# Longer runs in the loads of v and q, the weights' loads on SyncE's queue, and a reciprocal root in eight instructions, in an attention and channel-mixing kernel on one core

## The chip, the cores and the metric

The kernel runs on one core of one Trainium2 chip. The metric is the device time of one execution in microseconds, as the median of several runs. One core has TensorE (PE, with weight loads shown as PEld), VectorE (DVE), ScalarE (ACT), GpSimd (POOL), and SyncE (SP), which here only issues DMAs. SP's and ACT's queues both feed the core's 16 DMA engines.

## What is computed

Normalized attention over 8 batches, 12 heads, 448 positions and 64 columns per head, and then a channel-mixing block on the attention's output x of width 768, with inner width 1024:

```python
q_n, k_n = rmsnorm(q, g_q), rmsnorm(k, g_k)        # x / sqrt(mean(x*x) + 1e-6) * g
scores = (q_n @ k_n.T) / 8
attn = exp(scores - max) / (sum + 1e-9)
x = (attn @ v), heads side by side                 # (8, 448, 768)
x_prev = x shifted by one position
xk, xr = mu_k * x + (1 - mu_k) * x_prev, mu_r * x + (1 - mu_r) * x_prev
k = relu(xk @ w_k);  out = sigmoid(xr @ w_r) * ((k * k) @ w_v)
```

q, k, v and the g factors arrive as float32, the weights and mu as float64. The result is float32.

## The kernel before, in words

**Units.** The heads of a batch are worked in pairs (48 in all, `pairs`) and quads of four heads (24, `quads`, u in the code). Position p of a head is split as p = 7 r + t: r (0 to 63) lies on a partition, and t (0 to 6) in the free dimension. Two heads share the 128 partitions.

**Precision.** Numbers that go through PE are split into a high and a low float16 part, and three products are added up (high by high, high by low, low by high). The first batch's attention (quads 0 to 2, `U32 = 3`) is done in float32 in place of that, with one product. The weights are turned from float64 to float32 by bit operations, scaled per column block by a power of two, and split.

**Steps of a quad.** `load` fetches k and q into tiles `qk` (in part lent room named `xk`). `stats` squares them on ScalarE into a `nat` tile, GpSimd adds the halves, VectorE reduces to 28 sums per partition (`sst`), scales them, and `rsqrt` computes the reciprocal root (`ss`, with `stm` as room) by a bit trick and three Newton steps. `preps` multiplies by it. For quads 0 to 5 (`PE_T = 6`), PE transposes the result (`turn`), and the copy out of PSUM multiplies k by the factor g, held as a column `gc`; from quad 6 on GpSimd multiplies by g (`G`), ScalarE and GpSimd write the high and low part, and a DMA transpose brings them into `stk`. g_q, g_k and the 1/8 are folded into one factor, which is scaled by a number `gm` so that its largest element is balanced; the same number goes into q's root.

**Attention.** `scores` makes groups of 128 query rows by 448 keys in PSUM (`sc`), `expo` takes the maximum on VectorE and the exponential on ScalarE, `split` writes high and low part into `nat`, and a DMA transpose (or PE, in every other of the first groups, `probs_pe`) brings them into `pT`. `vload` fetches v of one pair (`vf`, two buffers) by four loads, `vprep` finds its scale (square, maximum over partitions by one small matmul, exponent bits) and writes high and low part (`vh`, `vl`). `attends` multiplies `pT` by v and copies the result out of PSUM into `x`.

**Channel mixing.** `wload` fetches forty half column blocks of the weights into `raw` (or lent room named `kk`), `weights` and `wsplit` convert them. `mix` forms xk and xr, `moe` multiplies, `square`, `gate` and `store` finish and write out. The first batch's `moe` cannot begin before the first weights are ready, and not end before all are.

**Order.** All of this is written as generators. A planner (`Plan`) holds a model of each engine's clock, of the DMAs and of each tile's last use; at each step it picks the generator whose next instruction could start first, less a priority (`PRIO_...`, `BOOST_...`, `MARGIN...`), and fixes that order on every engine. So the program is one static list for each engine. A waiting instruction holds all behind it on its engine, and a DMA that waits holds all behind it on its queue. Since all operations are issued by one helper, the profile gives nearly all of them the line L272.

In the kernel before, SP issues the loads of k, q and v, the transposes and the stores; ACT issues three of the first quad's loads, the forty weights' loads and the two of mu.

Of the kernel before, what the change touches and what calls it, by code (L numbers as in the profile page):

```python
# [16 lines left out]
P = 128  # L17
# [7 lines left out]
NH = D_MODEL // 2  # L25
TINY = 2.0 ** -60
RELU_SCALE = 2.0 ** -23.5
NEWTON = 3
# [12 lines left out]
VF_BUFS = 2  # L41
# [4 lines left out]
PRIO_P = 200  # L46
PRIO_S = 150
PRIO_A = 50
PRIO_Q = 50
PRIO_V = 310  # L50
MARGIN = 600
MARGIN_A = 400
MARGIN_V = 1200
# [5 lines left out]
PRIO_O = 300  # L59
# [3 lines left out]
BOOST_R = 500  # L63
BOOST_A = 0
BOOST_W = 300
BOOST_Q = 600
SLACK_S = 3
SLACK_Q = 2
# [6 lines left out]
PRIO_L = 0  # L75
# [3 lines left out]
V_SIDE = 2  # L79
SWITCH = 600  # L80
# [5 lines left out]
BOOST_F = 4000  # L86
# [8 lines left out]
W_GAP = 10e3  # L95
W_PUSH = 0.03
NEWTON_ON = "DVE"
# [18 lines left out]
def heads(tile_, off):  # L116
    ap = tile_[:, :, :]
    return bass.AP(tensor=ap.tensor, offset=ap.offset + off, ap=[list(ap.ap[0]), [HD, 2], [2 * HD, NT], [1, HD]])
# [86 lines left out]
class Plan:  # L205
    LAT = 35

    def __init__(self, tc):
        self.tc = tc
        self.clk = dict.fromkeys(("PE", "DVE", "ACT", "POOL", "SP"), 0.0)  # L210
        self.last, self.use, self.threads = {}, {}, []
        self.form, self.dma_free, self.acc, self.n = None, {"SP": 0.0, "ACT": 0.0}, False, 0
        self.held = {"DVE": [], "POOL": []}

# [51 lines left out]
    def emit(self, ops):  # L266
# [18 lines left out]
        elif ops[0].fn.__name__.startswith("dma"):  # L285
            op = ops[0]
            x = op.kw["out"]
            n = width(x) * x.ap[0][1]
            if "transpose" in op.fn.__name__:
                w, iss, tot = n / 128 * 1.21, 1600, 4000  # L290
            else:
                w, iss, tot = n / 55, 640, 3300
            w, tot = w * DMA_SLOW, tot * DMA_SLOW
            other = "ACT" if e == "SP" else "SP"
            if e == "ACT":
                end = s + (375 if n > 60000 else 610)
            else:
                end = max(s + iss, min(self.dma_free[e] - 1200, s + 4000))
# [5 lines left out]
            self.note(op, self.dma_free[e] + 900)  # L304
        else:
# [99 lines left out]
def rsqrt(V, y, a, t, pool=None):  # L405
    ti = t.bitcast(I32)
    yield V.tensor_scalar(out=ti, in0=a.bitcast(I32), scalar1=1, scalar2=None, op0=ALU.logical_shift_right)
    yield V.tensor_scalar(out=y.bitcast(I32), in0=ti, scalar1=-1.0, scalar2=float(0x5F3759DF), op0=ALU.mult, op1=ALU.add)
    for _ in range(NEWTON):
        if pool:  # L410
            yield pool.tensor_tensor(out=t, in0=a, in1=y, op=ALU.mult)
            yield pool.tensor_tensor(out=t, in0=t, in1=y, op=ALU.mult)
            yield pool.tensor_scalar(out=t, in0=t, scalar1=-0.5, scalar2=1.5, op0=ALU.mult, op1=ALU.add)
            yield pool.tensor_tensor(out=y, in0=t, in1=y, op=ALU.mult)
        else:
            yield V.tensor_tensor(out=t, in0=a, in1=y, op=ALU.mult)
            yield V.scalar_tensor_tensor(out=t, in0=t, scalar=-0.5, in1=y, op0=ALU.mult, op1=ALU.mult)
            yield V.scalar_tensor_tensor(out=y, in0=t, scalar=1.5, in1=y, op0=ALU.add, op1=ALU.mult)


def attn_moe_kernel(tc, q, k, v, g_q, g_k, mu_k, mu_r, w_k, w_v, w_r, out):
# [22 lines left out]
    gc = const.tile([P, 1], F32, name="gc")  # L444
# [8 lines left out]
    ones = const.tile([P, 1], F32, name="ones")  # L453
    WS = {}
# [4 lines left out]
    NQ, NPAIR, NSS, NSL = len(quads), len(pairs), 4 * NT, (NT + 1) // 2  # L459
    VFREE = [const.tile([P, 2 * NSL, HD], F32, name="vf%d" % n) for n in range(VF_BUFS)]  # L460

# [17 lines left out]
    def late():  # L479
# [11 lines left out]
        "vh": Ring(ap_, [P, 2 * NSL, HD], F16, "vh", VH_BUFS, plan),  # L491
        "vl": Ring(ap_, [P, 2 * NSL, HD], F16, "vl", VH_BUFS, plan),
# [39 lines left out]
    def setup():  # L532
        yield SP.dma_start(out=gq, in_=g_q.partition_broadcast(P))
        yield SP.dma_start(out=gk, in_=g_k.partition_broadcast(P))
        yield A.copy(out=ident16, in_=ident)
        yield V.memset(out=ones, value=1.0)
        for vf in VFREE:
            yield G_.memset(out=vf[HD:P, NSL - 1, :], value=0.0)
            yield G_.memset(out=vf[0:HD, NSL, :], value=0.0)
        st["vf"] = True  # L540
        yield V.scalar_tensor_tensor(out=G, in0=gq, scalar=1.0 / float(HD) ** 0.5, in1=gk, op0=ALU.mult, op1=ALU.mult)
        yield V.tensor_reduce(out=gm[:, 0:1], in_=G, axis=AX.X, op=ALU.max, apply_absolute_value=True)
# [3 lines left out]
        for h in range(2):  # L546
            hs = slice(h * HD, (h + 1) * HD)
            yield V.tensor_tensor(out=gd[hs, :], in0=G[hs, :], in1=ident[hs, hs], op=ALU.mult)
        yield V.tensor_reduce(out=gc, in_=gd, axis=AX.X, op=ALU.add)
        yield V.tensor_tensor(out=gm[:, 2:3], in0=gm[:, 1:2], in1=gm[:, 1:2], op=ALU.mult)  # L550
        yield V.tensor_scalar(out=gm[:, 3:4], in0=gm[:, 2:3], scalar1=1.0 / HD, scalar2=None, op0=ALU.mult)
        yield V.tensor_scalar(out=gm[:, 4:5], in0=gm[:, 2:3], scalar1=1e-6, scalar2=None, op0=ALU.mult)
        st["gm"] = True

    def mu_stats():
        yield from until(lambda: st["lu"] >= 1 and len(WFT))
        yield A.dma_start(out=mu[:, 0, 0, :], in_=mu_k.rearrange("(t p) -> p t", p=P))
        yield A.dma_start(out=mu[:, 1, 0, :], in_=mu_r.rearrange("(t p) -> p t", p=P))
        yield V.tensor_scalar(out=mu[:, :, 1, :], in0=mu[:, :, 0, :], scalar1=-1.0, scalar2=1.0, op0=ALU.mult, op1=ALU.add)
        u = small.tile([P, 2, ND], F32, name="muu")  # L560
        u2 = small.tile([P, 2, ND], F32, name="muu2")
        col = small.tile([P, 2], F32, name="mucol")
# [6 lines left out]
        m = small.tile([P, 1], F32, name="allmax")  # L569
# [7 lines left out]
    def load():  # L577
        for u in range(NQ):
# [3 lines left out]
            for n, src in enumerate((k, q)):  # L582
                t = yield from R["qk"].get(u < 3)
                for x in range(2):
                    D = (A if u == 0 and (x or n == 0) else SP).dma_start
# [3 lines left out]
                    else:  # L589
                        tf = t.rearrange("p h c -> p (h c)")  # L590
                        for t0 in range(x, NT - 1, 2):
                            o = t0 // 2 * 4 * HD
                            yield D(out=tf[x * HD:(x + 1) * HD, o:o + 4 * HD].rearrange("p (h d) -> p h d", d=HD),
                                    in_=src[b, 4 * j:4 * j + 4].rearrange("h (r t) d -> r h t d", t=NT)[:, :, t0, :])
                        yield D(out=tf[x * HD:(x + 1) * HD, 12 * HD:].rearrange("p (h d) -> p h d", d=HD),
# [7 lines left out]
    def stats():  # L603
        for u in range(NQ):
            st["su"] = u
            yield from until(lambda: u in LD and (st["gm"] or u < PE_T))
            y = small.tile([P, NSS], F32, name="ss", bufs=3)
            ss = small.tile([P, NSS], F32, name="sst", bufs=3)
            tm = small.tile([P, NSS], F32, name="stm", bufs=3)
            for n, t in enumerate(LD[u]):  # L610
# [3 lines left out]
                yield A.activation(out=xs, in_=tv, func=AF.Square)  # L614
# [8 lines left out]
            yield from rsqrt(V, y, ss, tm, NEWTON_ON == "POOL" and G_)  # L623
            SS[u] = y

    def preps():
        for u in range(NQ):
# [4 lines left out]
            for n, t in enumerate(LD.pop(u)):  # L632
# [13 lines left out]
                nat = yield from R["nat"].get(u < 3)  # L646
                if n:
# [6 lines left out]
                R["qk"].put(t)  # L654
                yield SP.dma_start_transpose(out=X[:, n], in_=nat.rearrange("p a c -> p (a c)"))
                R["nat"].put(nat)
            TQ[u] = X
            st["tq"] = u + 1

    def turn(w, X, n, u):  # L660
# [554 lines left out]
```

## Time and profile before

| what | value |
|---|---|
| median of 3 runs | 1036.73 us (1035.93 to 1038.05) |
| the profiled execution, first to last instruction | 1038.0 us |
| PE busy | 935.8 us, 90% of the span |
| VectorE busy | 788.0 us, 76% |
| ScalarE busy | 749.4 us, 72% |
| GpSimd busy | 661.0 us, 64% |
| mean granted TensorE clock | 0.970 |
| DMA packets | 447,043, of them 418,784 under 512 B |

How to read it: the span is that of the one profiled execution, from 0 to 1038.0 with 0.24 us ahead of its first instruction; it stands beside the longest of the three runs (1038.05), 1.3 us above their median. A busy share over the whole span is a mean over stages that have different limits. Idle time in front of an instruction is put down to what released it last. Matmuls overlap each other, so their summed durations are more than PE's busy time.

### The profile page before, as it was taken

The numbers are of one execution on the slowest core, as the hardware profiler recorded it, in microseconds if no ns is written. First come the engines' busy times: TensorE is split into PE (matmuls) and PEld (weight loads), VectorE is DVE, ScalarE is ACT, GpSimd is POOL, SyncE is SP. The second block draws the span as 40 slices with busy tenths as digits, with TensorE's granted clock in tenths as the row PEclk, the third lists the DMA queues.
The fourth block names the chain that finished last, engine by engine and source line by source line (L and its number), as shares of the span: only waits on it lengthen the run. The fifth ranks groups of instructions, "written<-read, shape, count | busy, mean of one in ns | idle before, by whom it ended". The sixth has DMA issues, their size and how long they took to land. (4 is left out here: it accounts for less than half of the span.)

```text
span 1038.0 us, 19082 instructions
## 1 busy us (share of the span) xinstructions
PE 935.8 (90%) x6262; PEld 495.5 (48%) x6262; DVE 788.0 (76%) x1973; ACT 749.4 (72%) x1755; POOL 661.0 (64%) x696
## 2 busy tenths in 40 slices
PE   1778677879999999999999999899989999999997
PEld 1444433435554555454545544455545554555564
DVE  4898879998978897978895988779876879673000
ACT  2787657997968887888887886987887787873311
POOL 2564658936678567877677757855984757646501
PEclk9898887989999999999999999999999999999999
DMA  8543437988897999789798798799869977771011
GB/s 198 143 122 106 115 91 166 202 160 155 156 174 125 176 183 161 139 156 179 157 175 140 152 185 167 129 171 183 173 118 159 170 154 135 139 140 32 1 31 31
DMA packets 447043, 146.63 MB, mean 141 GB/s; under 512 B 418784, under 2 KB 443360, under 8 KB 446944
## 3 DMA queue, kind: packets, MB, share of 16 engines
q1 hardware_dynamic: 427408, 127.42, 65.7%
q10 hardware_dynamic: 19536, 18.00, 6.1%
q8 instruction: 49, 0.80, 0.3%
q14 instruction: 50, 0.41, 0.1%
HBM read 50.40 MB, written 11.01 MB: 59 GB/s over the span
## 5 line engine op out<-in xcount | busy, mean ns | idle before, releaser
L272 PE MATMUL mm<-wvh,kk 128*128 128x384 f16 x896 | 233.8, 326 | 0.6 <-POOL kk L272 0.4
L272 ACT ACTIVATE sc<-sc,sums 128x448 f32<-128x448 f32 x294 | 180.9, 617 | 59.2 <-DVE sums L272 54.8
L272 DVE TENSOR_REDUCE sums<-sc 128x1 f32<-128x448 f32 x336 | 194.8, 614 | 28.7 <-PE sc L272 27.9
L272 PE MATMUL mm<-xk,wkh 128*128 128x448 f16 x768 | 209.0, 354 | 3.8 <-ACT kf L272 2.6
L272 DVE SCALAR_TENSOR_TENSOR nat<-sc,sums,nat 128x448 f16<-128x448 f32 x246 | 161.2, 675 | 29.1 <-ACT nat L272 28.6
L272 ACT ACTIVATE nat<-sc,sums 128x448 f16<-128x448 f32 (+1 forms) x278 | 168.7, 648 | 14.2 <-DVE sums L272 4.9
L272 PE MATMUL mm<-wrh,xr 128*128 128x384 f16 x672 | 177.6, 329 | 0.0
L272 PEld LDWEIGHTS <-kk 128*128 128x128 f16 (+1 forms) x1362 | 129.5, 98 | 96.3 <-issue 14.4
L272 PE MATMUL sc<-stk 64*128 64x448 f16 (+3 forms) x1104 | 131.7, 385 | 22.1 <-DVE nat L272 12.7
L272 PE MATMUL mm<-wvl,kk 128*128 128x384 f16 x448 | 146.0, 326 | 0.0
L272 PE MATMUL mm<-xk,wkl 128*128 128x448 f16 x384 | 135.8, 354 | 0.0
L272 PEld LDWEIGHTS <-xr 128*128 128x128 f16 x1008 | 96.1, 98 | 73.9 <-issue 14.4
L272 PE MATMUL ot<-pT,vh 128*64 128x448 f16 x672 | 103.3, 364 | 11.1 <-DMA pT<-nat 7.4
L272 PE MATMUL mm<-wrl,xr 128*128 128x384 f16 x336 | 110.3, 328 | 0.0
L272 PEld LDWEIGHTS <-wkh 128*128 128x128 f16 x768 | 72.1, 98 | 79.1 <-issue 18.4
L272 DVE SCALAR_TENSOR_TENSOR o<-o,mm 128x384 f32<-128x384 f32 x56 | 30.7, 548 | 88.5 <-PE mm L272 58.5
L272 POOL TENSOR_TENSOR o<-o,bsc 128x384 f32<-128x384 f32 x48 | 42.9, 894 | 82.0 <-DVE o L272 49.3
L272 POOL TENSOR_TENSOR qk<-qk,ss 128x896 f32<-128x896 f32 x36 | 63.3, 1757 | 44.4 <-DVE ss L272 36.7
L272 ACT ACTIVATE o<-mm,bsc 128x128 f32<-128x128 f32 x144 | 44.6, 382 | 50.8 <-PE mm L272 38.6
L272 PEld LDWEIGHTS <-stk 64*128 64x128 f16 x1008 | 36.1, 98 | 80.2 <-issue 50.7
L272 DVE SCALAR_TENSOR_TENSOR df<-x,bsc,df 128x448 f32<-128x448 f32 x68 | 63.2, 941 | 5.4 <-POOL df L272 5.3
L272 POOL TENSOR_TENSOR nat<-nat 128x448 f32<-128x448 f32 x38 | 44.5, 1170 | 35.1 <-ACT nat L272 35.0
(169 smaller groups left out, 1784.5 us busy)
## 6 DMA issues: line engine op xcount, KB each, us to landing
out_dram<-o SPq DMA_DIRECT2D x56, 192.0 KB, 3.3
qk<-in_k_dram SPq DMA_DIRECT2D x46, 224.0 KB, 3.8
qk<-in_q_dram SPq DMA_DIRECT2D x108, 64.0 KB, 2.5
vf<-in_v_dram SPq DMA_DIRECT2D x96, 64.0 KB, 2.7
raw<-in_moe_w_v_dram ACTq DMA_DIRECT2D x12, 512.0 KB, 4.9
vf<-in_v_dram SPq DMA_DIRECT2D x96, 48.0 KB, 2.4
raw<-in_moe_w_r_dram ACTq DMA_DIRECT2D x12, 384.0 KB, 3.4
kk<-in_moe_w_k_dram ACTq DMA_DIRECT2D x8, 384.0 KB, 4.4
```

The costliest lines, as they stand in the source:

```text
L272: r = op.fn(op.kw["out"], op.kw["value"]) if op.fn.__name__ == "memset" else op.fn(**op.kw)
```

## The change

- **v**: loaded, squared and scaled by quads and not by pairs, from quad 3 on with one scale for the quad. One buffer `vf` of double size takes the place of two. Each load takes four or three neighbouring t of a row of the split (1024 or 768 B in one run) where it took single ones (256 B). High and low part of a pair lie in one tile, `vhl`.
- **q from quad 6 on**: three neighbouring t of a head in one run (768 B), and the seventh by itself; four loads a quad, not eight.
- To keep the columns in step, `turn`, the high and low parts in `preps`, and the copy in `attends` use another order of t; the latter two need two instructions where there was one.
- **Queues**: the weights' and mu's loads, and q's second half of quad 0, are issued by SP. The loads of g_q and g_k come after those of the first quad.
- **g**: in batch 0 (quads 0 to 2) the factor is used without the balancing number, so `stats` of these quads does not wait for it.
- **Root**: `rsqrt` in eight instructions, not eleven; the scaling of the sums is done in the Square, and one addition of `eps` is left.
- The small tiles `ss`, `sst`, `stm` and `dg` come from rings that the planner knows; the planner gets a limit of eight DMAs in flight, other DMA costs, and other priorities.

```diff
-VF_BUFS = 2
+VF_BUFS = 1
...
-W_GAP = 10e3
+W_GAP = 6679.939
 class Plan: def emit
+            if len(self.flying) == DMA_LANES:
+                s = max(s, self.flying.pop(0))
...
-def rsqrt(V, y, a, t, pool=None):
...
+def rsqrt(V, y, a, t):
+    yield V.tensor_scalar(out=y.bitcast(I32), in0=a.bitcast(I32), scalar1=-0.5, scalar2=float(0x5F3759DF), op0=ALU.mult, op1=ALU.add)
+    yield V.tensor_tensor(out=t, in0=a, in1=y, op=ALU.mult)
+    yield V.tensor_tensor(out=t, in0=t, in1=y, op=ALU.mult)
+    yield V.scalar_tensor_tensor(out=t, in0=t, scalar=-10.0 / 3, in1=t, op0=ALU.add, op1=ALU.mult)
+    yield V.scalar_tensor_tensor(out=y, in0=t, scalar=5.0, in1=y, op0=ALU.add, op1=ALU.mult)
+    yield V.tensor_tensor(out=t, in0=a, in1=y, op=ALU.mult)
+    yield V.scalar_tensor_tensor(out=t, in0=t, scalar=-27.0 / 1024, in1=y, op0=ALU.mult, op1=ALU.mult)
+    yield V.scalar_tensor_tensor(out=y, in0=t, scalar=9.0 / 16, in1=y, op0=ALU.add, op1=ALU.mult)
 def setup
+        yield from until(lambda: 0 in LD)
         yield SP.dma_start(out=gq, in_=g_q.partition_broadcast(P))
         yield SP.dma_start(out=gk, in_=g_k.partition_broadcast(P))
...
+        yield V.tensor_reduce(out=gc[:, 0:1], in_=gd, axis=AX.X, op=ALU.add)
+        st["gc"] = True
...
+        yield V.tensor_tensor(out=gc[:, 1:2], in0=gc[:, 0:1], in1=gm[:, 1:2], op=ALU.mult)
 def mu_stats
-        yield A.dma_start(out=mu[:, 0, 0, :], ...
+        yield SP.dma_start(out=mu[:, 0, 0, :], ...
 def load
-                    D = (A if u == 0 and (x or n == 0) else SP).dma_start
+                    D = (A if u == 0 and n == 0 else SP).dma_start
...
-                        for t0 in range(x, NT - 1, 2):
-                            o = t0 // 2 * 4 * HD
-                            yield D(out=tf[x * HD:(x + 1) * HD, o:o + 4 * HD].rearrange("p (h d) -> p h d", d=HD),
-                                    in_=src[b, 4 * j:4 * j + 4].rearrange("h (r t) d -> r h t d", t=NT)[:, :, t0, :])
+                        w = NLO * HD
+                        yield D(out=tf[xs, 0:4 * w].rearrange("p (h c) -> p h c", h=4),
+                                in_=src[b, 4 * j:4 * j + 4].rearrange("h (r t) d -> r h (t d)", t=NT)[:, :, x * w:(x + 1) * w])
 def stats
-                yield A.activation(out=xs, in_=tv, func=AF.Square)
+                yield A.activation(out=xs, in_=tv, func=AF.Square, scale=gm[:, 6:7] if n and u >= U32 else HD ** -0.5)
...
-            yield from until(lambda: st["gm"])
-            yield V.tensor_scalar(out=ss[:, 0:2 * NT], in0=ss[:, 0:2 * NT], scalar1=1.0 / HD, scalar2=1e-6, op0=ALU.mult, op1=ALU.add)
-            yield V.tensor_scalar(out=ss[:, 2 * NT:NSS], in0=ss[:, 2 * NT:NSS], scalar1=gm[:, 3:4], scalar2=gm[:, 4:5], op0=ALU.mult, op1=ALU.add)
+            if u < U32:
+                yield V.tensor_scalar(out=ss, in0=ss, scalar1=1e-6, scalar2=None, op0=ALU.add)
+            else:
+                yield from until(lambda: st["gm"])
+                yield V.tensor_tensor(out=ss, in0=ss, in1=eps, op=ALU.add)
 def preps
-                yield A.copy(out=hi, in_=t4)
-                yield E_.tensor_tensor(out=lo, in0=t4, in1=hi, op=ALU.subtract)
+                for t4, hi, lo in views:
+                    yield A.copy(out=hi, in_=t4)
+                for t4, hi, lo in views:
+                    yield E_.tensor_tensor(out=lo, in0=t4, in1=hi, op=ALU.subtract)
 def vload
-        for i in range(NPAIR):
+        for u in range(NQ):
...
-                    yield SP.dma_start(out=vf[e * HD:(e + 1) * HD, o:o + n, :], in_=src[h][:, t::2, :])
+                    yield SP.dma_start(out=vf[e * HD:(e + 1) * HD].rearrange("p (x c) d -> p x (c d)", x=2)[:, :, o * HD:(o + n) * HD],
+                                       in_=src[:, :, t * HD:(t + n) * HD])
 def vprep
+        if half:
+            hl = yield from R["vhl"].get()
+            yield A.activation(out=hl.rearrange("p a c d -> p (a c) d").bitcast(BF16), in_=vf, func=AF.Square, accum_out=vs[:, 0:1])
...
+            for e in range(2):
+                if e:
+                    hl = yield from R["vhl"].get()
+                ve = vf[:, 2 * NSL * e:2 * NSL * (e + 1), :]
+                yield A.activation(out=hl[:, 0], in_=ve, func=AF.Copy, scale=sv)
+                yield V.scalar_tensor_tensor(out=hl[:, 1], in0=ve, scalar=sv, in1=hl[:, 0], op0=ALU.mult, op1=ALU.subtract)
 def attends
-            for lo, hi in ((0, NT),) if i % 2 == 0 else ((NT - 1, NT), (0, NT - 1)):
...
+            yield A.activation(out=x[:, 1:NT, :].rearrange("p (a t) c -> p t a c", a=2), in_=av[:, o:o + (NT - 1) * HD].rearrange("p (t a c) -> p t a c", a=2, c=HD), func=AF.Copy, ...
+            yield A.activation(out=x[:, NT, :], in_=av[:, o:o + HD], func=AF.Copy, ...
 def wload
-                yield A.dma_start(out=raw[:, 0:hk, :], in_=w[i * P:(i + hk) * P, ...
+                yield SP.dma_start(out=raw[:, 0:hk, :], in_=w[i * P:(i + hk) * P, ...
```

The rest of the constants, not shown: `PRIO_P` 200 to 429, `PRIO_S` 150 to 159, `PRIO_A` 50 to 37, `PRIO_V` 310 to 295, `MARGIN` 600 to 560, `MARGIN_A` 400 to 305, `MARGIN_V` 1200 to 569, `PRIO_O` 300 to 161, `PRIO_L` 0 to 165, `BOOST_R` 500 to 816, `BOOST_W` 300 to 248, `BOOST_Q` 600 to 898, `SLACK_S` 3 to 4, `SLACK_Q` 2 to 3, `SWITCH` 600 to 404, `BOOST_F` 4000 to 3894. A priority counts a tenth of its value in nanoseconds (`PS = 0.1`); `W_GAP` is the pace, in nanoseconds per column block, at which the weights' priority rises.

More of the change, by code (lines that the diff above doesn't have):

```diff
@@ L25 @@
 NH = D_MODEL // 2
+NSL = (NT + 1) // 2
+NLO = NT // 2
+KORD = [t // 2 + NSL * (t % 2) for t in range(NT)]
+QORD = [t // 2 + NLO * (t % 2) for t in range(NT - 1)] + [NT - 1]
 TINY = 2.0 ** -60
 RELU_SCALE = 2.0 ** -23.5
-NEWTON = 3
+DMA_LANES = 8
 MX = 4 + 2 * ND
@@ L606, in stats @@
             yield from until(lambda: u in LD and (st["gm"] or u < PE_T))
-            y = small.tile([P, NSS], F32, name="ss", bufs=3)
-            ss = small.tile([P, NSS], F32, name="sst", bufs=3)
-            tm = small.tile([P, NSS], F32, name="stm", bufs=3)
+            ss = yield from R["sst"].get()
             for n, t in enumerate(LD[u]):
@@ L711, in vfree @@
+            VF[u] = vf
+    def vfree(u, vf):
+        FR[u] = FR.get(u, 0) + 1
+        if FR[u] == 3:
             VFREE.append(vf)
     def vpreps():
-        i = 0
-        while i < NPAIR:
-            st["vi"] = i
-            n = V_SIDE if i < 2 * U32 else 1
-            yield from vprep([i + e for e in range(n)])
-            i += n
-    def vprep(js):
-        b, hp = pairs[js[0]]
-        n, half = len(js), js[0] >= 2 * U32
-        if hp == 0:
-            BS[b] = small.tile([P, 2 * NP], F32, name="bstat", bufs=3)
+        for u in range(NQ):
+            st["vi"] = u
+            yield from vprep(u)
@@ L726, in vprep @@
+    def vprep(u):
+        b, j = quads[u]
+        half = u >= U32
+        n = 1 if half else 2
+        NS = NP // 2 * n
+        if j == 0:
+            BS[b] = small.tile([P, 2 * NS], F32, name="bstat", bufs=3)
         s_ = BS[b]
         vs = small.tile([P, 4], F32, name="vs", bufs=4)
-        vh = vl = pt = None
-        for e, i in enumerate(js):
-            yield from until(lambda: i in VF and st["tq"] >= GATE_V)
-            vf = VF.pop(i)
-            if half:
-                vh = yield from R["vh"].get()
-                vl = yield from R["vl"].get()
-                sq = vh.bitcast(BF16)
-            else:
-                VV[i] = vf, None, None
-                pt = pt or (yield from banks["ot"].get())
-                sq = pt.rearrange("p (a c) -> p a c", c=HD)
-            yield A.activation(out=sq, in_=vf, func=AF.Square, accum_out=vs[:, e:e + 1])
-            if not half:
-                vfree(i, vf)
-                if e < n - 1:
-                    banks["ot"].put(pt)
-                    pt = None
@@ L746, in vprep @@
-        pt = pt or (yield from banks["ot"].get())
+        yield from until(lambda: u in VF and st["tq"] >= GATE_V)
+        vf = VF.pop(u)
+        hl = pt = None
+        if half:
+            hl = yield from R["vhl"].get()
+            yield A.activation(out=hl.rearrange("p a c d -> p (a c) d").bitcast(BF16), in_=vf, func=AF.Square, accum_out=vs[:, 0:1])
+            pt = yield from banks["ot"].get()
+        else:
+            for e in range(2):
+                VV[2 * u + e] = vf[:, 2 * NSL * e:2 * NSL * (e + 1), :], None, vf
+            pt = yield from banks["ot"].get()
+            for e in range(2):
+                yield A.activation(out=pt.rearrange("p (a c) -> p a c", c=HD), in_=vf[:, 2 * NSL * e:2 * NSL * (e + 1), :], func=AF.Square, accum_out=vs[:, e:e + 1])
+            vfree(u, vf)
@@ L1041, in wsplit @@
         sci = sc.bitcast(I32)
-        dg = small.tile([P, P], F32, name="dg", bufs=1)
+        dg = yield from R["dg"].get()
         yield V.tensor_tensor(out=dg, in0=pg[:, 0:P], in1=ident, op=ALU.mult)
         yield T.matmul(form=("f", 400), out=pg[:, P:2 * P], lhsT=ones.broadcast_to([P, P]), rhs=dg, start=True, stop=True)
+        R["dg"].put(dg)
         yield V.tensor_reduce(out=sc, in_=pg[:, P:2 * P], axis=AX.X, op=ALU.max)
```

190 lines of the change are left out of this document (96 added, 94 removed).

## The prediction

> **What bounds the kernel now.** I read the page first, then the busy time by stages, then PE's waits in the steady stage, then the first 25 us instruction by instruction, and last the groups of VectorE inside the front stage alone. The page gives the span, the packets, and the queue that nearly all of them are on (packets, MB, share of 16 DMA engines over the span):
>
> ```profile
> span 1038.0 us, 19082 instructions
> ...
> DMA packets 447043, 146.63 MB, mean 141 GB/s; under 512 B 418784, under 2 KB 443360, under 8 KB 446944
> ...
> q1 hardware_dynamic: 427408, 127.42, 65.7%
> ```
>
> The stages (length, then busy us of PE, PEld, DVE, ACT, POOL, then clock, DMA share, GB/s):
>
> ```profile
> 0.00:13.00 13.00, 0.00 (x0) 0.00 (x0) 2.23 (x14) 3.37 (x4) 2.09 (x11) 1.00 0.69 180
> 13.00:26.00 13.00, 3.20 (x15) 2.90 (x16) 10.72 (x31) 3.55 (x9) 3.53 (x6) 1.00 0.93 217
> 26.00:130.00 104.00, 80.81 (x520) 46.11 (x518) 91.75 (x272) 76.94 (x182) 61.26 (x66) 0.90 0.44 121
> 130.00:156.00 26.00, 18.47 (x110) 8.98 (x109) 18.99 (x55) 13.28 (x27) 15.38 (x20) 0.83 0.34 94
> 156.00:208.00 52.00, 40.14 (x269) 20.76 (x270) 48.87 (x109) 45.05 (x97) 45.46 (x49) 0.87 0.84 184
> 208.00:234.00 26.00, 19.36 (x135) 9.75 (x134) 24.93 (x72) 23.41 (x53) 7.92 (x11) 0.88 0.82 159
> 234.00:884.00 650.00, 625.43 (x4289) 324.36 (x4285) 541.28 (x1318) 522.01 (x1236) 459.87 (x463) 0.99 0.86 159
> 884.00:1026.00 142.00, 142.00 (x897) 79.04 (x896) 48.38 (x106) 60.93 (x148) 63.87 (x73) 1.00 0.32 63
> 1026.00:1038.00 12.00, 6.34 (x40) 3.62 (x37) 0.81 (x2) 0.89 (x3) 1.66 (x2) 0.95 0.13 33
> ```
>
> There are three regimes. From 234 us on, PE is the bound: it is busy 625.43 of 650 us and then without a gap to 1026. From 13 to 234 us VectorE is the bound: 10.72 + 91.75 + 18.99 + 48.87 + 24.93 = 195.3 us of 221, 0.88, while PE idles 59 us. Before 13 us nobody works: VectorE is busy 2.23 us, PE not at all. So what the change saves counts before 234 us if it lies on VectorE or at the start; after 234 us only PE's own work and the stalls of 650 - 625.43 = 24.6 us count. What releases PE there (total us, times, longest):
>
> ```profile
> PE ot L272 <- DMA pT<-nat: 6.6, 8, 1.4
> PE sc L272 <- DVE nat L272: 5.3, 9, 1.2
> PE sc L272 <- DMA stk<-nat: 4.0, 4, 2.6
> ```
>
> **Term 1, the start.** The chain to PE's first instruction, from the timeline, and the landing time of the first k loads:
>
> ```profile
> 0.73 1.40 ACTq L272 DMA_DIRECT2D xk<-in_k_dram  x2
> 2.45 11.90 SPq L272 DMA_DIRECT2D vf<-in_v_dram  x8
> 9.04 2.01 ACTq L272 DMA_DIRECT2D raw<-in_moe_w_k_dram  x2
> 11.10 0.95 ACT L272 ACTIVATE xk<-xk 128x896 f32<-128x896 f32 x1 [7.34 <-DMA kk<-in_moe_w_k_dram]
> 13.29 0.62 DVE L272 TENSOR_REDUCE sst<-xk 128x14 f32<-128x448 f32 x1 [2.59 <-POOL xk L272]
> 16.42 0.61 DVE L272 TENSOR_REDUCE sst<-nat 128x14 f32<-128x448 f32 x1
> 20.06 1.09 DVE L272 TENSOR_TENSOR nat<-xk,ss 128x896 f32<-128x896 f32 x1
> 21.30 1.73 PE L272 MATMUL sc<-ident,nat 128*128 128x128 f32 x7 [21.30 <-DVE nat L272]
> ...
> xk<-in_k_dram ACTq DMA_DIRECT2D x2, 224.0 KB, 6.2
> ```
>
> ScalarE's Square of k starts at 11.10, just behind two weights' loads that its own queue issues from 9.04 to 11.05. The k loads were issued by 2.13 and land after 6.2 us, at about 8.3. With those issues on SyncE the Square can start some 3 us earlier. The second reduce (16.42) comes 3.1 us behind the first, although its Square follows the other by 0.95: between them VectorE runs the balancing chain of g. Quads 0 to 2 no longer need it, which frees 2.1 us. From the end of the second reduce (17.03) to the multiply (20.06) run 13 small instructions, 0.233 us each; nine remain, 0.9 us less. Together 6.0, so PE would start at 15.3. I take -5, because both halves of q now go through SyncE and g is loaded behind them; the ends are 0 and -6.0.
>
> **Term 2, VectorE in the front.** Its groups between 0 and 234 us, with seven quads' reciprocal roots in them (busy us, mean ns):
>
> ```profile
> L272 DVE SCALAR_TENSOR_TENSOR ss<-stm,ss 128x28 f32<-128x28 f32 x20 | 6.2, 312 | 0.5
> L272 DVE TENSOR_TENSOR stm<-sst,ss 128x28 f32<-128x28 f32 x21 | 4.1, 197 | 0.5
> L272 DVE SCALAR_TENSOR_TENSOR stm<-stm,ss 128x28 f32<-128x28 f32 x21 | 4.1, 196 | 0.5
> L272 DVE TENSOR_SCALAR sst<-sst,gm 128x14 f32<-128x14 f32 x7 | 3.7, 526 | 0.0
> L272 DVE TENSOR_SCALAR sst<-sst 128x14 f32<-128x14 f32 x7 | 2.3, 324 | 0.0
> L272 DVE TENSOR_SCALAR ss<-stm 128x28 int32<-128x28 int32 x7 | 1.7, 237 | 0.2
> L272 DVE TENSOR_SCALAR stm<-sst 128x28 int32<-128x28 int32 x7 | 1.5, 208 | 0.1
> ```
>
> The two scalings (3.7 + 2.3) become one addition, which I price like the 0.197 row: 7 x 0.2 = 1.4, so 4.6 are saved. The shift goes: 1.5. Nine steps of the iteration become seven: 14.4 us for 62 instructions is 0.232 each, 14 fewer are 3.2. For v, quads 3 and up do in one pass what two pairs did:
>
> ```profile
> L272 DVE TENSOR_REDUCE vs<-ot 128x1 f32<-128x128 f32 x42 | 11.8, 280 | 6.2 <-PE ot L272 6.2
> L272 PE MATMUL ot<-ident,vs 128*128 128x128 bf16 x48 | 10.6, 234 | 1.3 <-ACT vh L272 0.5 <-ACT x L272 0.5 <-ACT ot L272 0.2
> ```
>
> One reduce (0.28) and three one-column instructions (0.2 each by the rows above) fall away per quad, for about 2.5 quads in the front: 2.2. The sum is 11.5 us of VectorE. If the front shortens by VectorE's share of it, 0.88, that is 10; I take -8, because from 130 to 156 us VectorE is busy only 18.99 of 26. The ends are 0 and -11.5.
>
> **Term 3, ScalarE's queue.** Here are the last of the forty weights' issues (twenty columns in two halves), and one issue on SyncE:
>
> ```profile
> 211.88 0.37 ACTq L272 DMA_DIRECT2D raw<-in_moe_w_v_dram  x1
> 59.95 0.59 SPq L272 DMA_DIRECT2D vf<-in_v_dram  x1
> ```
>
> Some 11 of the 0.37 us issues lie between 156 and 234 us, where ScalarE is busy 68.5 of 78 us: 4.1 us there, of which I take -1, since VectorE is busier in the same stretch (73.8). The ends are 0 and -4.1. SyncE gets 42 issues, and loses 96 of v's 192 and 72 of q's 144: 126 fewer, by 0.59 some 74 us off its queue, nearly all behind 130 us.
>
> **Term 4, PE.** v's maxima cost 27 matmuls and not 48. 21 x 0.234 = 4.9, but neighbouring matmuls overlap, and a few of the 21 lie where PE idles anyway: -3, ends 0 and -4.9.
>
> **Term 5, the steady stage's stalls.** v's and q's rows of 256 B become runs of 1024 and 768 B: v 43,008 packets to 12,288, q (from quad 6) 32,256 to 13,824, so 49,152 of 447,043 go, 11%. On that queue a packet takes 0.657 x 1038 x 16 / 427,408 = 25.5 ns, so at most 78 us on each of 16 engines, whose share is 0.86 in this stage. Of the stalls the DMAs release 6.6 + 4.0 = 10.6; what goes there lets VectorE's (5.3) come next. I take -3, with ends of -10.6 and +7 (the other 14 us grow by half, as the new priorities order everything anew; they add no instruction, and this is where I put their price).
>
> **Term 6, what is added.** k's and q's high and low parts are written in two pieces (18 quads, 36 tiles), and the result of an even pair in two, too:
>
> ```profile
> L272 ACT CAST nat<-qk 128x896 f16<-128x896 f32 x28 | 27.0, 965 | 3.8 <-POOL qk L272 2.1 <-POOL x L272 1.6
> L272 ACT CAST xk<-df 128x448 f16<-128x448 f32 x34 | 19.5, 578 | 5.8 <-DVE df L272 5.6
> L272 POOL TENSOR_TENSOR nat<-qk,nat 128x896 f16<-128x896 f32 x28 | 53.6, 1914 | 18.4 <-ACT nat L272 16.4 <-DVE nat L272 1.6
> L272 POOL TENSOR_TENSOR kk<-kf,kk 128x448 f16<-128x448 f32 x46 | 49.5, 1077 | 1.3
> L272 ACT ACTIVATE x<-ot,bstat 128x64 f32<-128x64 f32 x21 | 7.0, 332 | 8.3 <-PE ot L272 8.3
> ```
>
> A second instruction costs ScalarE 2 x 0.578 - 0.965 = 0.19, 6.9 in all, and GpSimd 2 x 1.077 - 1.914 = 0.24, 8.6 in all; the 24 extra copies cost at most 0.332 each, 8.0. ScalarE (522 of 650) and GpSimd (460 of 650) have room under PE in the steady stage. I take +1; without that cover it would be all 23.5. One v buffer of double size in place of two: its load has a quad's time, 650 / 18 = 36 us, against 6.2 for the slowest landing above, so 0; it only costs if the buffer is given back later than 30 us into its quad, and then each of 18 quads pays the excess.
>
> **The sum.** -5 - 8 - 1 - 3 - 3 + 1 = -19, from 1038.0 to 1019.0. The profiled execution stands 1.3 above the median of 1036.73, so the forecast is 1017.7. All the good ends together: 37.1 less than the median, 1000.
>
> **Rivals.**
> (a) The weights set the end of the front, not VectorE's load. The last of forty loads goes out at 211.88, one per 5.3 us, and PE is full only 22 us later. If that pace stays, terms 1 to 3 are lost, and -3 - 3 + 1 is left: 1031.7. For it: each load waits for a buffer that a chain over four engines gives back. Against it: VectorE is in that chain, and is busy 0.88 of the time.
> (b) The DMAs are what holds the steady stage, and the front converts in full: all good ends, 1000. For it: the share of 0.86 in that stage, and 418,784 of 447,043 packets under 512 B. Against it: only 10.6 us of waits name a DMA, and the transposes' packets stay. The Trainium skill's "DMA: Bandwidth & Descriptors", section Specifications, says that line rate wants at least 512 B per transfer; by that rule the new runs of 768 and 1024 B all come out on the good side, and the result would be this one. The trace bears it out so far as q1's packets take 25.5 ns for a mean of 298 B.
> (c) Slower: SyncE's queue becomes the bound of the front. A weights' load that waits for its buffer now holds the loads of k, q and v and the transposes behind it. The trace has such a queue: eight v loads take it 11.90 us, 1.49 each against 0.59 for one alone. At 0.9 us more for each of forty loads the front gets 36 longer: 1036.7 - 19 + 36 = 1053.7. It decides from 19 / 40 = 0.48 us per load on. Against it: one load per 5.3 us is a light stream, and half of v's issues leave the queue. The Trainium skill's "Perfetto Trace Analysis", section DMA Optimizations, advises to balance DMAs over the engines that can issue them where descriptor generation is the bottleneck; the change does the opposite, and by that advice this rival would be the likely one. The 1.49 us per issue are the only sign of it here.
>
> **How the numbers follow.** No change means within 0.2% (about 2 us), about what a measurement of this kernel can tell. Forecast 0.55; (a) 0.21, of which 0.04 within 0.2%; (b) 0.10; (c) 0.14, of which 0.03 within 0.2% and 0.11 slower. So faster 0.82, same 0.07, slower 0.11. The range goes from 1001 (most of (b) outside) to 1036: what is left out is (c) and half of (b), under 2 in 10.
>
> **What would show it.** PE's first instruction near 16 us (term 1; still at 20 if q's or g's loads are late). PE full from about 220 us and not 234, with VectorE's busy time before it some 11 us lower (terms 1 to 3). Some 398,000 packets, and less than 10.6 us of PE's waits on transposes (term 5). 27 matmuls of v's maxima (term 4). I am wrong if the last weights' load still goes out near 212 us, if SyncE's waits stand in front of late k and q loads, or if PE's idle time between there and the last matmul grows beyond 25 us, since the order written by the planner is another one.

## The result, and the profile after

The changed kernel takes 1001.66 us (median of 4 runs, 1000.64 to 1003.88) against 1037.39 for the kernel before on the same chip: a ratio of 0.965 (0.9627 to 0.9673). The forecast was 1017.7, the range 1001 to 1036. The profiled execution spans 998.9 us, 39.1 less than the one before. Slow executions are left out below (one of 1018 us with the weights on ScalarE, one of 3299 us of the kernel before), but one of 1067 us, at a granted clock of 0.89, is in the row of the short runs and raises its median by 0.7 us. From the page of the changed kernel, its span and its DMAs:

```profile
span 998.9 us, 18675 instructions
...
DMA packets 395201, 146.61 MB, mean 147 GB/s; under 512 B 345440, under 2 KB 391520, under 8 KB 395104
...
q1 hardware_dynamic: 394816, 144.95, 72.4%
```

The stages of the changed kernel (columns as in the prediction):

```profile
0.00:13.00 13.00, 0.00 (x0) 0.00 (x0) 1.75 (x6) 4.75 (x7) 3.80 (x13) 1.00 0.72 191
13.00:26.00 13.00, 7.00 (x24) 4.14 (x24) 11.25 (x40) 3.31 (x8) 2.81 (x4) 1.00 0.44 130
26.00:130.00 104.00, 83.93 (x550) 50.48 (x552) 94.88 (x274) 79.54 (x189) 66.60 (x74) 0.89 0.50 140
130.00:156.00 26.00, 18.66 (x120) 8.73 (x117) 21.63 (x45) 14.48 (x26) 22.67 (x27) 0.79 0.58 167
156.00:208.00 52.00, 44.12 (x293) 22.85 (x292) 47.55 (x108) 45.83 (x101) 36.23 (x38) 0.97 0.73 158
208.00:234.00 26.00, 26.00 (x197) 13.31 (x195) 22.61 (x62) 24.71 (x62) 12.00 (x17) 1.00 0.80 153
234.00:884.00 650.00, 639.57 (x4420) 325.69 (x4418) 548.63 (x1243) 551.63 (x1325) 492.37 (x523) 1.00 0.89 167
884.00:999.00 115.00, 109.25 (x649) 63.22 (x647) 14.72 (x22) 23.23 (x58) 37.70 (x41) 0.99 0.10 25
```

PE is full from 208 us on, 26 us earlier. The 39.1 us come from three places. PE's idle time before 234 us fell from 234 - 162.0 = 72.0 to 234 - 179.7 = 54.3 us (-17.7). Its idle time from 234 to 884 us fell from 24.6 to 10.4 (-14.2). Its busy time as a whole fell from 935.8 to 928.5 (-7.3, which goes with the granted clock: see term 4). Behind 884 us it idles 5.7 us in both. The start, from the timeline, with the last weights' load:

```profile
1.92 0.72 ACTq L275 DMA_DIRECT2D xk<-in_k_dram  x1
9.15 0.95 ACT L275 ACTIVATE xk<-xk 128x896 f32<-128x896 f32 x1 [6.82 <-DMA xk<-in_k_dram]
11.34 0.62 DVE L275 TENSOR_REDUCE sst<-xk 128x14 f32<-128x448 f32 x1 [10.41 <-POOL xk L275]
12.66 0.60 DVE L275 TENSOR_REDUCE sst<-nat 128x14 f32<-128x448 f32 x1
15.60 1.09 DVE L275 TENSOR_TENSOR nat<-xk,ss 128x896 f32<-128x896 f32 x1
16.84 1.73 PE L275 MATMUL sc<-ident,nat 128*128 128x128 f32 x7 [16.84 <-DVE nat L275]
...
180.04 0.38 SPq L275 DMA_DIRECT2D raw<-in_moe_w_v_dram  x1
```

What releases PE between 234 and 884 us now (total us, times, longest). The DMA transposes, 10.6 us before, are down to 1.4 in these two rows and 0.3 in one more:

```profile
PE sc L275 <- DVE nat L275: 2.4, 4, 0.9
PE ot L275 <- ACT vhl L275: 2.1, 2, 1.9
...
PE ot L275 <- DMA pT<-nat: 0.9, 2, 0.7
PE sc L275 <- DMA stk<-nat: 0.5, 1, 0.5
```

The surprise is why the transposes are in time. The 16 DMA engines worked hardly less: (0.657 + 0.061) x 1038.0 = 745 us each before, 0.724 x 998.9 = 723 after. What has more room is SyncE's own queue. These are its issues between 234 and 884 us (duration of one issue in ns, min/median/max; first and last start), first before, then after:

```profile
L272 SPq DMA_DIRECT2D qk<-in_q_dram x136: 602/615/1452, 245.5 to 854.9; - x136
L272 SPq DMA_DIRECT2D vf<-in_v_dram x138: 595/616/1560, 233.7 to 883.4; - x138
L272 SPq DMA_TRANSPOSE pT<-nat x98: 1322/1956/3709, 235.7 to 869.9; - x98
```

```profile
L275 SPq DMA_DIRECT2D qk<-in_q_dram x64: 601/616/1340, 268.6 to 797.5; - x64
L275 SPq DMA_DIRECT2D vf<-in_v_dram x72: 595/656/1704, 251.6 to 843.4; - x72
L275 SPq DMA_TRANSPOSE pT<-nat x104: 1295/1690/4148, 237.2 to 870.7; - x104
```

A load takes the queue 0.6 us as a rule, for 48 KB as for 224 KB, and a transpose 1.3 to 4 us. Added up one by one from the trace, the queue's issues take 566 of these 650 us before (502 issues) and 498 after (375). In gaps of more than 0.5 us, in which the queue waits for data or has nothing to do, it spends 50 us before and 110 after. The loads and stores make the difference: their issues take 254 us before and 167 after, the transposes' 313 and 333. A transpose's issue is no constant: in the changed kernel its median is 2.1 us right behind another transpose and 1.5 us behind a gap. SyncE is never shown as busy on the page, so this was not seen.

### The profile page after: what moved, and what is told of

The parts are those of the page before. It is cut to its first block, busy times and chain, and to the rows that moved or that the text cites. A ratio compares the mean times of both kernels' runs of the same rounds, so it can differ in the third digit from the quotient of the medians.

```text
span 998.9 us, 18675 instructions
## 1 busy us (share of the span) xinstructions
PE 928.5 (93%) x6241; PEld 488.4 (49%) x6241; DVE 763.0 (76%) x1794; ACT 747.5 (75%) x1771; POOL 674.2 (67%) x732
## 2 busy tenths in 40 slices
DMA packets 395201, 146.61 MB, mean 147 GB/s; under 512 B 345440, under 2 KB 391520, under 8 KB 395104
## 3 DMA queue, kind: packets, MB, share of 16 engines
q1 hardware_dynamic: 394816, 144.95, 72.4%
## 5 line engine op out<-in xcount | busy, mean ns | idle before, releaser
L275 ACT ACTIVATE sc<-sc,sums 128x448 f32<-128x448 f32 x294 | 183.7, 628 | 38.9 <-DVE sums L275 33.5
L275 DVE TENSOR_REDUCE sums<-sc 128x1 f32<-128x448 f32 x336 | 197.3, 613 | 13.8 <-PE sc L275 13.4
L275 ACT ACTIVATE nat<-sc,sums 128x448 f16<-128x448 f32 (+1 forms) x270 | 160.7, 650 | 32.6 <-DVE sums L275 14.8
L275 PE MATMUL mm<-wrh,xr 128*128 128x384 f16 x672 | 175.6, 327 | 0.0
L275 DVE SCALAR_TENSOR_TENSOR nat<-sc,sums,nat 128x448 f16<-128x448 f32 x238 | 152.6, 676 | 25.5 <-ACT nat L275 24.9
L275 PEld LDWEIGHTS <-xr 128*128 128x128 f16 x1008 | 96.1, 98 | 72.0 <-issue 10.6
L275 PE MATMUL ot<-pT,vhl 128*64 128x448 f16 x1008 | 103.4, 355 | 2.5 <-DVE vs L275 1.5
L275 POOL TENSOR_TENSOR o<-o,bsc 128x384 f32<-128x384 f32 x48 | 45.0, 938 | 79.3 <-DVE o L275 60.9
L275 ACT ACTIVATE o<-mm,bsc 128x128 f32<-128x128 f32 x144 | 45.4, 395 | 62.7 <-PE mm L275 44.7
L275 PEld LDWEIGHTS <-vhl 128*64 128x64 f16 x1008 | 54.6, 110 | 47.7 <-issue 11.9
L275 DVE SCALAR_TENSOR_TENSOR df<-x,bsc,df 128x448 f32<-128x448 f32 x68 | 72.0, 1068 | 7.4 <-POOL df L275 7.1
```

The costliest lines, as they stand in the source:

```text
L275: r = op.fn(op.kw["out"], op.kw["value"]) if op.fn.__name__ == "memset" else op.fn(**op.kw)
```

## The experiments

The first four runs set out from another theory, "Order" in their expectations: the planner's new order brings the steady stage's gain. The second of them spoke against it (within 2 us expected, 44 measured). The theory since then is that the number of issues on SyncE holds the transposes up and not the size of the packets. Its rivals: the packets; the weights' move; VectorE's root; or the planner's new order. "Order kept" marks a kernel in which every engine has the changed kernel's own order, the edit being made when an instruction is emitted; "planned anew" lets the planner see the edit. (Shares of the queue above 0.9 in an expectation were summed over merged rows of the timeline, which take in the gaps between issues; issue by issue they are 0.87 before and 0.77 after.) All results in one table; idle and load times are of the profiled executions. The kernels ran on three more chips, each beside the kernel before, so a difference between two rows is taken from their ratios, times 1037.

| kernel | us | ratio to before (interval) | PE idle 0-234 | PE idle 234-884 | last weights' load |
|---|---|---|---|---|---|
| before | 1037.39 | 1 | 72.0 | 24.6 | 211.9 |
| after | 1001.66 | 0.965 (0.9627-0.9673) | 54.3 | 10.4 | 180.0 |
| short runs, old issues | 1053.71 | 1.0161 (1.0115-1.0207) | 56.4 | 49.1 | 180.1 |
| long runs, old issues | 1047.93 | 1.0077 (1.0049-1.0106) | 55.0 | 45.2 | 179.8 |
| the same, planned anew | 1106.92 | 1.0662 (1.0619-1.0705) | 59.1 | 82.7 | 173.6 |
| weights on ScalarE | 1004.21 | 0.9664 (0.9637-0.9691) | 53.9 | 11.7 | 180.2 |
| longer root | 1026.36 | 0.9875 (0.9848-0.9903) | 61.3 | 21.5 | 189.1 |
| the same, planned anew | 1040.38 | 1.0018 (0.9996-1.004) | 67.3 | 19.1 | 179.2 |
| after, old constants | 1022.33 | 0.9831 (0.9808-0.9853) | 72.1 | 12.0 | 214.3 |
| before, new constants | 1088.16 | 1.0476 (1.0436-1.0516) | 66.3 | 62.7 | 203.7 |
| after, one margin moved | 1025.75 | 0.988 (0.9845-0.9914) | 63.8 | 13.8 | 173.8 |
| before, one margin moved | 1039.14 | 0.9992 (0.9976-1.0008) | 71.5 | 23.7 | 220.4 |
| before, merged loads | 1025.24 | 0.985 (0.9827-0.9873) | 74.3 | 13.6 | 213.3 |
| fewer issues still | 1087.2 | 1.0448 (1.0424-1.0472) | 51.8 | 61.8 | 178.4 |

**Issues against packets.** Both kernels are the changed one, order kept. In the second, v's and q's long-run loads are cut into the old number of issues; in the first, into 256 B runs as well (which leaves these elements in another order of t).

```diff
 load, order kept
-    yield D(out=..., in_=...)                 # q: one load of four heads
+    yield cut(D(out=..., in_=...), [...])     # long runs: heads 0-1, 2, 3; short: t = x, x+2, x+4
 vload, order kept
-    yield SP.dma_start(out=..., in_=...)      # v: two heads, x = 0, 1
+    yield cut(SP.dma_start(...), [...])       # one piece for each x
```

> The changed kernel with v's and q's loads cut back to runs of 256 B and to the old number of issues (eight per quad for each), every engine's order kept as it is; the elements land in another order of t, so the output is another one. Theory Order (the steady stage's gain of 14 us comes from the new priorities and the new DMA costs, which set the order): at most +3 us, PE's idle time from 234 us on stays near 10 us. Rival DMA (short packets and full queues held the steady stage): +10 us or more, most of it as PE's waits on the transposes into pT and stk, which come back to some 10 us.

> As the run before, but the cut loads keep long runs (1024, 768 B), so that only the number of issues on SyncE's queue is the old one; output unchanged. Theory Order: within 2 us of the changed kernel. Rival DMA, by the issues: as slow as the run with 256 B. Rival DMA, by the packets: within 2 us here and +10 us there.

The issues alone cost 0.0427 of the time before, 44 us; the short runs on top of them, measured on the same chip, 5.8 us or 0.6 to 0.8%, although they bring the packets back to the old number. Stage, PE's waits in it, and q1, of the kernel with long runs and old issues:

```profile
234.00:884.00 650.00, 604.82 (x4102) 307.05 (x4101) 513.67 (x1181) 520.01 (x1243) 458.97 (x483) 0.98 0.85 160
```

```profile
PE sc L281 <- DMA stk<-nat: 17.2, 9, 3.6
PE sc L281 <- DMA stk<-natx: 7.9, 4, 2.5
...
PE ot L281 <- DMA pT<-nat: 3.3, 2, 1.9
```

```profile
q1 hardware_dynamic: 397504, 144.96, 69.2%
```

The front is as in the changed kernel. The steady stage stalls 34.8 us more, and the rows of transposes grow by some 28 of these. The DMA engines work 0.692 x 1047.1 = 725 us, as after (723). So the same bytes in nearly the same packets (397,504 on this queue for 394,816) are late when they and the transposes come through a fuller queue: its issues take 569 of the 650 us again.

The same edit planned anew is far slower, but from other waits (PE's waits over the whole run):

> v's and q's loads cut as in the run on issues (old number of issues, long runs), but now the planner counts each issue and orders all engines anew. If the issues themselves cost the 4.5% seen with the order kept (SyncE's queue is too full), most of it stays: +30 us or more over the changed kernel. If the loss came from an order that did not allow for them, a new order hides most of 135 issues of 0.6 us: at most +10 us.

```profile
PE sc L275 <- DVE nat L275: 46.8, 23, 15.6
PE ot L275 <- ACT vhl L275: 43.9, 11, 13.5
...
PE ot L275 <- DMA pT<-nat: 1.2, 1, 1.2
```

The transposes are in time here, and the queue's issues take 494 of the 650 us, no more than in the changed kernel. What is late is, among others, v's parts (`vhl`): between 234 and 884 us ScalarE, which writes them, waits 19.1 us for v's loads to land, while the queue waits only 3.6 us for v's buffer. So the loss of over 30 us came as expected, but not through a full queue. This run shows that a queue with room doesn't make the stage fast by itself; it neither supports the theory nor refutes it.

**The other way round.** The kernel before, its order kept, with only v's loads merged over two heads and q's three 256 B loads into one: 168 issues fewer, nearly the same bytes (128.98 MB on this queue for 127.42), in longer runs (the elements arrive in another order of t).

```diff
 vload of the kernel before, order kept
-    four loads a pair, x192          (64 KB, runs of 256 B)
+    in_=v[b, 2 * hp:2 * hp + 2].rearrange("h (r t) d -> r h (t d)", ...)     x96, 128 KB
```

> The kernel before, with v's loads merged by heads (two per pair, not four) and q's three 256 B loads merged into one, in long runs: 168 issues fewer on SyncE's queue, nearly the same bytes, everything else and all order as in the kernel before. The elements land in another order of t (and the zero rows of v are overwritten), so the output is another one. Theory Queue (SyncE's issues hold the steady stage; its queue is busy 94% of it): 8 to 15 us faster than before, PE's idle time from 234 to 884 us falls from 25 to about 12 us, its waits on DMA transposes near 2 us. Theory Order (only a matched order of all engines gains): within 3 us of before.

It gains 1.5%, and all of it in the steady stage, where its row and its waits on transposes come near the changed kernel's:

```profile
234.00:884.00 650.00, 636.37 (x4375) 329.11 (x4376) 548.50 (x1342) 534.40 (x1267) 473.15 (x474) 0.99 0.87 165
```

```profile
PE ot L280 <- DMA pT<-nat: 1.0, 1, 1.0
PE sc L280 <- DMA stk<-nat: 1.0, 1, 1.0
```

Its front gains nothing. With the order kept, the theory holds in both directions. How much of this 1.5% is due to its longer runs (375,568 packets on the queue for 427,408) was not separated; the 0.6 to 0.8% between the two kernels above is the nearest measure of it.

**Weights on ScalarE, order kept.** `SP.dma_start` back to ScalarE's queue for the weights and mu.

> The changed kernel with the weights' and mu's loads issued from ScalarE's queue again, each at the place in ScalarE's order where SyncE issued it in time, all other order kept. If ScalarE's issues cost the front what the prediction said (term 3): +1 us, at most +4. Rival: ScalarE's own stream stands at loads whose buffer is not yet free, as it did from 9.04 to 11.05 us before: +8 us or more, all ahead of 234 us.

0.0014 slower than the changed kernel, 1.5 us (2.6 by the medians), which the two overlapping intervals can't tell from none.

**A longer root.** Four more of the small instructions in each root (100 more on VectorE), which change no value; first order kept, then planned anew.

```diff
 rsqrt
     yield V.tensor_tensor(out=t, in0=a, in1=y, op=ALU.mult)
+    yield V.tensor_tensor(out=t, in0=a, in1=y, op=ALU.mult)     # and three more such repeats
```

> The changed kernel with four of the root's instructions on VectorE issued again (same operands, same result) in each quad, so 13 small instructions per quad as before, all order kept. Term 2 says that VectorE's time ahead of 234 us converts at about 0.7 to 0.9: four more by 0.25 us in seven quads are 7 us of VectorE, so +5 us, all in the front, and PE's steady stage unchanged. Rival (VectorE has slack in the front too, another chain ends it): under +2 us.

> Four more small VectorE instructions per root, as in the run on the root, but counted by the planner, which orders all engines anew. With the order kept they cost some 23 us, more than their own 24 x 1 us. If it is VectorE's time in the front: +5 us. If every quad's chain to the transposes pays: +15 us or more. If only the old order did not allow for them: about 0.

The expectation was 5 us, all in the front. Order kept it costs 23 us, a little more than the 21.9 us by which VectorE's busy time grows (763.0 to 784.9): PE idles 7.0 us more in the front and 11.1 more in the steady stage, where VectorE was thought to have room. So in a static list an instruction in front of a result that PE waits for can count there too. Planned anew the loss is 38 us; the two differ by the order alone.

**The constants.** The changed code with the old priorities, margins and pace of the weights (its new model of the DMAs kept); the old code with the new ones and the model; and one margin moved by 20 in either kernel.

```diff
 after, old constants                    before, new constants: the reverse
-PRIO_P = 429 ... W_GAP = 6679.939
+PRIO_P = 200 ... W_GAP = 10e3
 after, one margin moved                 before, one margin moved
-MARGIN = 560                            -MARGIN = 600
+MARGIN = 580                            +MARGIN = 620
```

> The changed kernel with all priorities, margins and paces of the kernel before (the planner's DMA costs stay the new ones). The mirror of the kernel before under the new constants (1088). If the removed work and issues are worth what the measured gain says whatever the order: near 1020, well under the 1088 of that mirror. If the match of constants and kernel is most of it: 1040 to 1080.

> The kernel before with the changed kernel's priorities, margins and DMA costs in its planner, and none of the other changes. Theory Order: the constants alone bring the steady stage's 14 us: about 1020. Rival (the removed work and issues bring it, the constants only fit it): 1030 to 1045, steady stage's PE idle time 20 us or more.

> The changed kernel with one constant moved a little (MARGIN 560 to 580), which gives another order of the same instructions: a measure of how much the order alone scatters. If the constants are a fine fit: +5 to +15 us. If any sane order does: within 3 us.

> The kernel before with MARGIN 600 moved to 620: how much another order costs it. If it is as finely fitted as the changed kernel (which lost 24 us by such a step): 1050 to 1065. If it is not: within 5 us of before, and then part of the measured gain is a better fit of the order.

The front and the steady stage of the changed code with old constants, and then of the old code with new ones:

```profile
0.00:234.00 234.00, 161.94 (x1036) 88.30 (x1038) 184.57 (x503) 162.98 (x363) 133.99 (x157) 0.90 0.61 145
234.00:884.00 650.00, 638.02 (x4394) 328.15 (x4390) 527.43 (x1221) 544.76 (x1302) 481.73 (x514) 0.99 0.86 164
```

```profile
0.00:234.00 234.00, 167.74 (x1075) 89.76 (x1079) 202.21 (x549) 166.70 (x371) 135.73 (x160) 0.90 0.62 145
234.00:884.00 650.00, 587.35 (x3950) 299.81 (x3943) 503.15 (x1212) 489.05 (x1147) 425.75 (x419) 0.95 0.80 149
```

This divides the gain. The steady stage's gain goes with the code: 12.6 of the 14.2 us come under the old constants as well. The front is neither's alone: under the old constants the new code gains nothing there (161.94 against 161.98), though VectorE works 13 us less; the old code gains 5.8 from the new constants, and loses 38 in the steady stage; together they gain 17.7. The margin moved by 20 takes 24 us from the changed kernel, 9.5 of it in the front, and nothing that can be measured from the kernel before. The 1022 us and the 1039 us were foreseen by one of the two sides of their expectations; the 1088 us and the 24 us lie beyond both sides of theirs.

**Fewer issues still.** The changed kernel, order kept, with 24 pairs of stores as one DMA each, and the first quad's k loads issued on ScalarE ahead of the copy that brings its table load.

```diff
 store, order kept
-    yield SP.dma_start(out=r[tt], in_=o[e * HD:(e + 1) * HD, :])            # e = 0, 1
+    out=r[tt:tt + 2], in_=o                                                 # 2 x 64 x 768, one DMA
```

> The changed kernel with two more steps of the same kind, all other order kept: 24 pairs of stores of the output go out as one DMA each (24 issues fewer on SyncE's queue), and ScalarE issues the first two k loads ahead of its first activation, at 0.7 us and not 1.9. Theory Queue: 2 to 5 us faster than the changed kernel (1.2 at the start, the rest in the steady stage and the tail). If the queue no longer binds: 1 us faster, by the start alone.

It was meant to beat both kernels and is the third slowest of all. The start came 2.2 us earlier than in the changed kernel, where 1.2 was expected; the steady stage did not (timeline, stage, PE's waits, transposes' issues):

```profile
14.62 1.73 PE L291 MATMUL sc<-ident,nat 128*128 128x128 f32 x7 [14.62 <-DVE nat L291]
```

```profile
234.00:884.00 650.00, 588.16 (x3926) 296.54 (x3924) 490.32 (x1122) 496.61 (x1187) 440.97 (x463) 0.96 0.95 152
```

```profile
PE ot L291 <- ACT vhl L291: 18.8, 6, 5.4
PE sc L291 <- DMA stk<-nat: 11.1, 3, 5.7
```

```profile
L291 SPq DMA_TRANSPOSE pT<-nat x93: 1374/2305/9144, 235.8 to 877.8; - x93
```

A transpose's issue now takes up to 9.1 us where 4.1 was the longest. The DMA share rises to 0.95 while GB/s falls from 167 to 152. The packets of the stores (3072 B each) say why: while any of them is under way between 240 and 870 us, 11.4 are on average in the changed kernel, 2.4 here. So the merged store keeps about two DMA engines busy. What is issued behind it waits: all 17 transposes' issues of more than 3.8 us (5.4 to 9.1) stand one or two places behind a merged store on the queue, and each ends within 0.3 us of the end of its last packet. The Trainium skill's "DMA: Bandwidth & Descriptors", section Why a DMA increments its semaphore by 16 and not by 1, says that the number of engines is the largest up to 16 that divides the slowest dimension of both sides, here 2; the 2.4 agree. The store was not tried without the earlier k loads, but those lie at 0.7 us, and the long issues all stand behind stores. So this run has fewer issues (331 in the stage, 375 in the changed kernel) and a fuller queue (552 of 650 us): the count alone does not decide.

## Why the prediction came out as it did

The sign and most of the rows to look for were right. The result lies 0.7 us inside the range, and that is luck: the sum was 20 us short of the 39 by which the profiled execution shrank, and terms 2 and 5 had other causes than those given.

| step | predicted | measured |
|---|---|---|
| terms 1 to 3, PE idle before 234 us | -14 | -17.7 |
| term 4, PE's work | -3 | -7.3 |
| terms 5 and 6, PE idle 234 to 884 us | -2 | -14.2 |

**Term 1.** PE starts at 16.84, 4.5 us earlier, against -5. The Square came at 9.15 and not near 8.1: the k loads went out at 1.92, behind ScalarE's table load, and the later one landed at 9.06. The landing at 8.3 in the prediction was drawn from the median of two loads, of which the later landed at 9.02. In the last experiment, where they go out at 0.73, the Square begins at 6.44. Further, the reduces are 1.3 us apart (1.0 expected), and nine instructions take 2.3 us and not 2.1.

**Term 2** failed as a mechanism, though the front gained even more than its sum. VectorE's share of the front was to turn its savings into time. With the old constants VectorE saves 13 us there, PE starts at 18.28 (3.0 us earlier than before), and the front gains none of it. What else held the front may be what rival (a) named, the weights, though no run followed that chain. In the kernel with old constants the last of their loads still goes out at 214.3, and in the changed one at 180.0; the five kernels with a last load behind 200 us idle 66 to 74 us in the front, the nine others 52 to 67. The change moves the pace: `W_GAP` from 10 to 6.68 us stands in the diff and had no price. It does not do so by itself, for in the old code all new constants together, `W_GAP` among them, bring the last load only to 203.7. Nor are early loads enough: they go out at 173.8 and 179.2 in two kernels that keep only 8.2 and 4.7 of the 17.7 us. What shortened the front stays open, but for the start. The row that was to show term 2, VectorE 11 us less busy before 234 us, is wrong: 199.67 for 197.50, since more of the work was done by then.

**Term 3** fits in size: -1 against 1.5 to 2.6 us of the weights put back on ScalarE, which the measurement can't tell from none. Rival (c) did not come: SyncE's queue had room in the front, where its issues take 91 of 234 us. The sign of it was misread, too: the 11.90 us of eight v loads are a merged row of the timeline, with gaps; issue by issue they take 0.6 us each, 4.8 in all. The Trainium skill's "Perfetto Trace Analysis", section DMA Optimizations, on balance over the issuing engines would have spoken for it; here 42 issues more on SyncE did no harm.

**Term 4.** v's maxima take 27 matmuls, as predicted. They explain at most the 4.9 us of the upper end. Work does not explain the rest: kernels with the same 6241 matmuls show PE busy from 928.5 to 950.8 us. What goes with it is the granted clock, whose mean is 0.970 before and 0.981 after, and 0.946 in the kernel with 950.8 us. Busy time multiplied by mean clock is 908 us before and 911 after, so PE's work did not measurably fall. A matmul `ot<-pT,vhl` takes 354 ns at the full granted clock and 581 at half of it (kernel with long runs and old issues). The steady stage has 10.8 us at half clock before, none after, 20.5 in that kernel, and 51.2 in the one with fewer issues still. Why the clock falls there was not tested.

**Term 5** is the step that fell short most. The packets came as counted (395,201 for some 398,000), and the transposes' waits went, 8.9 of the 10.6 us. But by the experiments the cause was mostly not v's and q's packets, and the ends were drawn from the rows that name a DMA, so that the other 14 us of stalls could only grow. They fell as well (to 8.7), and fell in the kernel before with merged loads (14.0 to 11.6), where nothing else was changed: what PE waits for from VectorE and ScalarE hangs on late transposes too, it seems, though no run followed such a chain. The prediction counted 126 issues, 74 us, off SyncE's queue in term 3, and gave them a price of nothing. It never asked how full this queue was.

**Term 6** stayed under its cover. These are the two pieces of a high part, and the extra copies, in the changed kernel:

```profile
L275 ACT CAST nat<-qk 128x768 f16<-128x768 f32 x14 | 12.3, 875 | 0.0
L275 ACT CAST nat<-qk 128x128 f16<-128x128 f32 x14 | 4.9, 351 | 0.0
L275 ACT ACTIVATE x<-ot,bstat 128x64 f32<-128x64 f32 x42 | 14.3, 341 | 0.0
```

A second piece costs 875 + 351 - 965 = 261 ns against 190, a copy 341 against 332. ScalarE rises to 552 of 650 us and GpSimd to 492. Of PE's waits in the stage, those on ScalarE grow from 1.0 to 3.1 us (`vhl` 2.1, `o` 1.0), and none on GpSimd is left. The wait for v's parts (`vhl`) is 43.9 us in the kernel planned anew with the old issues, where v's loads come late: the cover depends on loads in time. Two buffers were not tried.

**Rival (b)** came nearest, with 1000 us, and its cause was wrong as well: the DMA engines' time fell by 22 us of the 78 that were its bound, and the short runs cost 5.8 us. By the Trainium skill's "DMA: Bandwidth & Descriptors", section Specifications, on 512 B per transfer, one would expect these runs to bring most of the gain; here the measurement decides against that.

**Not separated:** how much of the 19 us of the constants (0.9831 to 0.965) is a lasting property of a better order, and how much an order that fell well. That a step of 20 in one margin costs 24 us speaks for the second.

## What to carry to other kernels

Add up the issue times of each DMA queue by stage before anything else is said of DMAs: a queue that the page never shows as busy can hold the whole stage. A load fills it by the issue and not by the byte; a transpose's issue also grows with what is under way ahead of it. A queue with room is not enough, as the kernel planned anew shows (494 of 650 us in the queue, PE idle 82.7). Merge transfers where that lowers the count, with a long outermost dimension: 64 served well here, 2 did not. Where a planner writes a static order, test each edit with the order kept, and price the order by itself: here one step of one constant moved the time by 24 us, two thirds of the whole change.

## What the runs showed of the hardware

Two of the findings were not expected. An issue takes SyncE's queue some 0.6 us (medians 0.62 and 0.66) for a v load of 64 or 48 KB as for one of 128 or 96 KB, and a transpose 1.3 to 4.1 us; so 168 issues fewer, in longer runs, were worth 1.5% with the DMA engines' time at 737 us each for 745. And a store of 384 KB whose outermost dimension is 2 kept 2.4 packets under way where two stores of 192 KB kept 11.4, which lengthened transposes' issues on the same queue to 9.1 us.
